# Linear attention block: denominators with heads on partitions, and reciprocals repeated by plain DMAs

## The chip, the cores and the metric

The kernel runs on one core of a Trainium2 chip. The metric is the device time of one execution in microseconds (us), as the median of several runs; lower is better.

## What is computed

An attention block and a feed-forward block, each behind a layer norm, with residuals. S = 2048 tokens, D = 512 features, 32 heads of 16 features, 1792 hidden features, all in bf16.

```
qkv = layernorm(x) @ wqkv
phi(t) = where(t > 0, t + 1, exp(t)) + 1e-6
kv  = einsum("bhsd,bhse->bhde", phi(k), v)
z   = sum of phi(k) over tokens
num = einsum("bhqd,bhde->bhqe", phi(q), kv)
den = einsum("bhqd,bhd->bhq", phi(q), z) + 1e-6
h   = x + (num / den) @ wo
out = h + relu(layernorm(h) @ w1) @ w2
```

The part at issue is 1 / den: one number for each token and head, by which all 16 features of that head are scaled.

## The kernel before

All tensors stay in SBUF. Tokens come in 16 tiles of 128 and in 4 chunks of 512 tokens. In the first third, each tile is normalized and transposed, K and the product G = ln^T phi(K) are accumulated over all tiles, and z is summed. Q is made transposed, with features on partitions: `pqT[c]` is 128 x 4 x 512, where the four blocks jb hold 8 heads of 16 features each. G, wv and wo are folded into one matrix `m_sb`, so attention's output is `h = x + (phi(q) / den) @ m_sb`. Then follow the hidden layer (`p` words, L510), its ReLU (`pA` on ACT, `pD` on VectorE) and the second product (`f` words, L530).

The order of everything is one list of words, `ORDER`, written out by hand: each word is an operation with its indices, the last one often a PSUM bank. Engines take their instructions in that order, and each waits for its data by semaphores; DMAs are issued by SP in that order too. A word that waits holds up all later words of its engine.

The denominators of a chunk c take this path. `zhd` holds z spread so that column q of block jb belongs to head q of that block (32 columns, of which 8 are not zero).

- `dn` (L443-451): sixteen matmuls with a 128 x 128 piece of `pqT[c]` as weights and 8 columns of `zhd` moving. Tokens come out on partitions, 128 numbers a partition.
- `dnl` (L453, ACT): Ln of these into `ld`.
- `dnx` (L459, ACT): Exp of minus that, read 16 times for each head, into `rn` (the memory of `wk_sb`), two token tiles at a time.
- `dt` (L478, SP): a transposing DMA for each token tile, from `rn` into `rd`, which then holds the reciprocal for each feature and token. Four a chunk. `rd` has room for one chunk.
- `dm` (L482, VectorE): `pqs = pqT * rd`, two blocks at once. It reads `rd` over all 512 tokens, so it needs all four transposes of the chunk.
- `h` (L490, L494, PE): four matmuls a token tile from `pqs` and `m_sb`; `hD` adds x.

Around chunk 1, SP's list goes on with a load of w2 (`l2.3.4`) and the transposes of `hn` (`x` words, L292), which the hidden layer needs.

Of the kernel before, what the change touches and what calls it, by code (L numbers as in the profile page):

```python
# [11 lines left out]
BF16 = mybir.dt.bfloat16  # L12
# [4 lines left out]

ORDER = """
const table lx.0.1 lx.2.1 S.0 lx.1.1 S.2 A.0 S.1 A.2 R.0.1 N.0 R.2.1 lx.3.1 lk.0.2 lx.4.2 masks warm.1.7
warm.9.7 A.1 R.1.1 T.0.6 S.3 warm.1.7 N.2 T.2.4 N.1 A.3 E.0 R.3.1 T.1.5 lk.2.2 S.4 E.1 N.3 A.4 V.2 S.5 A.5  # L20
K.0.6 lx.6.2 K.1.3 T.3.1 F.0.1 U.0.1 lx.8.4 E.3 K.2.0 M.0.1 S.6 D.0.1 K.3.2 A.6 S.7 F.1.1 M.1.1 lx.12.4 R.4.2
N.5 A.7 N.4 U.1.1 D.1.1 F.2.1 U.2.1 R.6.2 S.8 S.9 N.7 A.9 A.8 M.2.1 N.6 lq.0.2 G.0 T.5.1 E.5 T.4.3 G.1 X.7
K.5.1 D.2.1 E.4 K.4.0 R.8.2 T.6.3 G.2 N.9 X.9 F.3.1 U.3.1 S.12 N.8 S.13 X.8 lq.2.2 M.3.1 A.13 A.12 D.3.1 E.6
K.6.2 F.4.2 R.12.2 U.4.2 K.7.3 G.3 M.4.2 S.11 F.6.2 U.6.2 N.12 D.4.2 S.10 S.14 N.13 M.6.2 A.11 A.10 D.6.2 A.14
R.10.2 X.12 K.9.1 G.4 N.11 S.15 N.10 A.15 X.13 K.8.0 G.5 G.6 za.2 U.8.2 F.8.2 X.11 X.10 G.7 R.14.2 K.13.1
K.12.0 M.8.2 N.15 D.8.2 za.4 N.14 K.11.3 K.10.2 G.8 l2.0.3 F.12.2 U.12.2 za.6 X.15 X.14 Q.0.0.0 F.10.2 Q.0.1.1
lv.2.2 l1.0.2 M.12.2 lv.0.2 l2.10.4 U.10.2 qU.0.0.2 qF.0.0.2 M.10.2 za.8 D.12.2 D.10.2 za.10 za.12 K.14.2 G.9
K.15.3 F.14.2 U.14.2 G.10 Q.0.3.1 Q.0.2.0 M.14.2 qF.0.2.2 qU.0.2.2 G.11 zf.12 D.14.2 G.12 z.0.2.14 z.2.2.14
z.1.2.14 z.3.2.14 qM.0.2.2 l2.7.3 lo.0.2 lo.2.2 l1.2.2 qM.0.0.2 qD.0.2.2 G.13 zc G.14 qD.0.0.2 zh dn.0.0 G.15
gD.2.2 gD.0.2 Q.1.1.3 Q.1.0.2 dnl.0 dnx.0.0.2 Q.1.2.0 dnx.0.2.2 kv.3.4 kv.0.4 kv.1.4 kv.2.4 Q.1.3.1 qF.1.0.2  # L30
qM.1.0.2 kx qF.1.2.2 qW.1.0.2 dt.0 dt.3 dt.2 dt.1 m.2.6 m.1.5 m.3.7 m.0.4 mA.0.2 Q.2.0.2 Q.2.1.3 qM.1.2.2
mA.2.2 qW.1.2.2 dn.1.5 dm.0.0.2 dm.0.2.2 dnl.1 dnx.1.2.2 Q.2.3.1 h.3.5 hD.3 h.0.6 h.1.7 hD.0 s.3 dnx.1.0.2
dt.6 Q.2.2.0 dt.4 dt.7 dt.5 qF.2.0.2 qU.2.0.2 h.2.6 hD.1 Q.3.0.2 Q.3.1.3 s.0 qF.2.2.2 qU.2.2.2 s.1 qU.3.0.2
a.3 a.0 hD.2 qM.2.0.2 n.0 a.1 n.1 dm.1.0.2 dm.1.2.2 n.3 s.2 Q.3.2.0 Q.3.3.1 qD.2.0.2 a.2 qM.2.2.2 n.2 qF.3.0.2
qF.3.2.2 l2.3.4 x.0 qM.3.2.2 qD.2.2.2 h.5.6 h.7.7 h.6.5 x.1 t.2.3 r.0.4 e.2 h.4.4 x.3 dn.2.3 dnl.2 dnx.2.0.2
p.0.0.2 dt.8 hD.6 qM.3.0.2 qW.3.2.2 hD.4 p.0.1.3 qD.3.0.2 hD.5 dnx.2.2.2 pA.0.0.2 p.0.3.1 p.0.2.0 dn.3.6
pD.0.2.2 p.0.5.3 p.0.4.2 pD.0.4.2 p.0.7.1 p.0.6.0 p.0.13.3 s.6 dt.10 p.0.12.2 dt.11 dt.9 hD.7 a.6 s.5 dm.2.0.2
dm.2.2.2 dnl.3 pA.0.6.2 a.5 pD.0.12.2 f.2.6.0.7 s.7 h.11.7 h.9.0 p.0.9.3 h.8.5 p.0.8.2 dnx.3.2.2 dnx.3.0.2
hD.9 a.7 hD.11 p.0.10.0 f.3.7.0.7 p.0.11.1 h.10.4 dt.15 pA.0.10.2 pD.0.8.2 dt.14 dt.13 dt.12 s.4 s.9 n.5
dm.3.2.2 s.11 hD.8 a.11 dm.3.0.2 hD.10 n.7 f.2.6.7.7 h.13.5 h.15.4 n.6 hD.15 a.4 n.4 s.8 h.14.1 f.3.7.7.7  # L40
h.12.2 f.0.4.0.7 x.5 x.6 s.10 hD.14 a.10 hD.13 hD.12 n.10 x.4 s.13 s.12 x.7 n.11 a.9 a.8 f.1.5.0.7 a.12 s.15
p.1.1.1 p.1.0.0 pA.1.0.2 f.1.5.7.7 a.15 s.14 fo.2 p.1.8.0 p.1.9.1 n.12 a.13 fo.3 n.15 n.13 fo.1 pD.1.8.2
f.0.4.7.7 a.14 n.8 p.1.12.0 p.1.13.1 p.1.2.2 p.1.3.3 p.1.10.6 r.12.4 r.4.4 pA.1.12.2 n.9 x.11 x.15 x.10 x.9
x.8 pD.1.2.2 p.1.7.5 p.1.5.1 fd.2 fd.3 p.1.4.0 p.2.3.3 p.2.2.2 n.14 fo.0 pD.1.4.2 pD.2.2.2 fd.0 x.13 x.14
p.2.0.0 p.1.11.7 p.2.7.3 p.2.1.1 r.8.4 pA.2.0.2 p.2.6.2 p.1.6.4 pD.2.6.2 p.2.4.0 pA.1.10.2 pA.1.6.2 p.2.5.1
pA.2.4.2 f.7.7.0.7 p.2.12.0 p.2.13.1 f.4.4.0.7 f.5.5.0.7 p.2.10.2 f.4.4.7.7 p.2.11.3 f.6.6.0.7 pD.2.10.2
pD.2.12.2 fd.1 x.12 f.6.6.7.7 f.5.5.7.7 p.2.8.0 p.2.9.1 p.3.2.2 p.3.3.3 fo.6 pD.2.8.2 fo.4 fo.5 p.3.4.0
f.7.7.7.7 p.3.5.1 pA.3.4.2 pD.3.2.2 fo.7 f.10.6.0.7 p.3.1.1 f.9.5.0.7 p.3.7.3 p.3.0.0 f.8.4.0.7 p.3.6.2 fd.6
f.9.5.7.7 f.11.7.0.7 f.10.6.7.7 fd.4 fd.5 fd.7 pA.3.0.2 pA.3.6.2 f.8.4.7.7 p.3.12.0 fo.9 f.11.7.7.7 p.3.13.1
p.3.11.3 p.3.10.2 pD.3.10.2 fo.8 fo.11 pA.3.12.2 p.3.9.1 f.13.5.0.7 p.3.8.0 f.12.4.0.7 pA.3.8.2 fo.10 fd.10  # L50
fd.9 f.13.5.7.7 f.14.6.0.7 fo.13 f.12.4.7.7 f.15.5.0.14.3.1 f.14.6.7.7 f.15.7.0.14.0.2 fd.13 fd.8 fd.11 fo.12
fo.14 fo.15.3.1 f.15.4.0.14.2.1 fd.12 fd.14 fd.15.3.1 fo.15.0.2 fo.15.2.1 fd.15.0.2 fd.15.2.1
"""


# [1 line left out]
def kernel(  # L57
# [10 lines left out]
    nc = tc.nc  # L68
    P = 128
    xf = A_x.flatten_outer_dims()  # L70
    of = out.flatten_outer_dims()
    S, D = xf.shape
    FF = B_w1.shape[1]
    H = 32
    DH = D // H
    NT = S // P
    CW = 512
    CT = CW // P
    NCH = S // CW
    KD = D // P  # L80
    KF = FF // P
    Q4 = P // KD
    QH = P // DH
# [5 lines left out]
    big = ctx.enter_context(tc.tile_pool(name="big", bufs=1))  # L89
# [47 lines left out]
    rd = big.tile([P, 4, CW], BF16, name="rd")  # L137
    pqs = big.tile([P, NQ, CW], BF16, name="pqs")
    hn = big.tile([P, NQ, D], BF16, name="hn")
    o_t = gT  # L140
    r4 = rd
    rn = wk_sb
    z_acc = acts[1][:, 0:4, :].rearrange("p a n -> p (a n)").bitcast(F32).rearrange("p (a n) -> p a n", a=2)
    zeros = m_sb[:, 0, :]
# [281 lines left out]
    def op_dx4(c):  # L426
        nc.scalar.activation(out=r4[:, c, :], in_=ld[:, c % 2, :], func=ACT.Exp, scale=-1.0)

    def op_rp(c, jb, b):
        at_bank["rp", c, jb] = b  # L430
        rows = slice(jb * Q4, (jb + 1) * Q4)
        nc.tensor.matmul(
            bk[:, b, :], lhsT=erep[rows, :], rhs=r4[rows, c, :], start=True, stop=True
        )
# [146 lines left out]
```

## Time and profile before

| what | value |
|---|---|
| median of 3 runs | 169.91 us (169.65 to 170.24) |
| the profiled execution: span, first to last instruction | 168.6 us; no other time of this execution is listed |
| TensorE busy | 163.1 us, 97% |
| VectorE busy | 104.7 us, 62% |
| ACT busy | 64.3 us, 38% |
| mean granted clock of TensorE | 0.999 |

In the rows of the timeline the first number is the start and the second the length, both in us; then follow engine, line, operation, operands, shapes and the number of instructions merged, and in brackets how long the engine was idle before and what ended that. PEld is the load of weights, which runs beside PE. In the chain of waits the columns are start, length and what the time went to. In a group's row, the columns behind the count are busy us and mean ns of one, and then the idle time before. In a row of one source line, three numbers with slashes are least, median and greatest ns. In a row by windows stand the window's length, the busy time of each engine with its instructions, the granted clock, the mean busy share of the 16 DMA engines, and GB/s.

### The profile page before, as it was taken

How to read it: one execution, taken by the hardware profiler on the slowest of the kernel's cores; microseconds unless marked ns; L12 is line 12 of the kernel's file. 1: busy time of each engine (PE TensorE's matmuls, PEld its weight loads, DVE VectorE, ACT ScalarE, POOL GpSimd, SP SyncE). 2: the span in 40 equal slices, each digit the busy share in tenths (PEclk: the TensorE clock that was granted, in tenths of full speed). 3: DMA queues.
4: the chain of work that ended last, by engine and by line, in shares of the span. 5: the costliest groups of instructions: out<-in, count | busy, mean ns of one | idle time of the engine just before them, and what ended most of it. 6: DMA issues, size and time to landing. Idle time of an engine off the chain costs nothing.

```text
span 168.6 us, 2307 instructions
## 1 busy us (share of the span) xinstructions
PE 163.1 (97%) x875; PEld 76.3 (45%) x875; DVE 104.7 (62%) x207; ACT 64.3 (38%) x97; POOL 4.8 (3%) x21
## 2 busy tenths in 40 slices
PE   7799999999999999999999999999999999999993
PEld 2354444444554354444444444444444444444463
DVE  3999999996879896978799725220066401007132
ACT  3699867775589755600201140170000203021000
POOL 7400000000000000000000000000000000000000
PEclk9999999999999999999999999999999999999999
DMA  4972847896414653232142343400000200000232
GB/s 130 295 254 47 146 79 176 312 365 230 95 31 93 156 97 79 45 74 50 41 83 40 62 90 100 91 4 0 0 0 31 93 4 0 0 0 0 79 111 62
DMA packets 30091, 15.36 MB, mean 91 GB/s; under 512 B 22656, under 2 KB 29056, under 8 KB 30080
## 3 DMA queue, kind: packets, MB, share of 16 engines
q1 hardware_dynamic: 30080, 15.21, 34.6%
q8 instruction: 7, 0.11, 0.3%
q14 instruction: 4, 0.03, 0.1%
HBM read 7.86 MB, written 2.10 MB: 59 GB/s over the span
## 4 chain that ended last, share of the span: by engine, by line
PE 84%; ACT 4%; DMA 4%; SPq 3%; DVE 2%; issue 1%; DVEq 0%; ACTq 0%
PE bk L530 29%; PE bk L510 29%; PE bk L351 7%; PE bk L299 7%; PE bk L494 6%; PE bk L307 5%; DMA wk_sb<-in_A_wqkv_dram 3%; ACT eb L317 1%; DMA rd<-wk_sb 1%; SPq L201 1%; SPq L480 1%; PE bk L448 1%; ACT rb L320 1%; DVE pqT L332 1%; ACT lnT L280 1%
## 5 line engine op out<-in xcount | busy, mean ns | idle before, releaser
L530 PE MATMUL bk<-w_sb,at 128*128 128x512 bf16 (+2 forms) x252 | 51.5, 355 | 0.0
L510 PE MATMUL bk<-lnT,w_sb 128*128 128x512 bf16 x224 | 51.4, 379 | 0.0
L516 ACT ACTIVATE at<-bk 128x1024 bf16<-128x1024 f32 x14 | 14.1, 1023 | 70.3 <-PE bk L510 70.3
L521 DVE TENSOR_SCALAR at<-bk 128x1024 bf16<-128x1024 f32 x14 | 17.0, 1221 | 33.7 <-PE bk L510 33.7
L530 PEld LDWEIGHTS <-at 128*128 128x128 bf16 x252 | 23.6, 98 | 25.2
L510 PEld LDWEIGHTS <-w_sb 128*128 128x128 bf16 x224 | 21.8, 98 | 26.0 <-issue 0.2
L538 DVE SCALAR_TENSOR_TENSOR gT<-bk,rstd,h_nat 128x512 bf16<-128x512 f32 (+2 forms) x18 | 12.0, 686 | 18.3 <-PE bk L530 15.9
L317 ACT ACTIVATE eb<-bk 128x1024 bf16<-128x1024 f32 (+1 forms) x18 | 16.5, 925 | 6.1 <-PE bk L299 3.5
L299 PE MATMUL bk<-wk_sb,lnT 128*128 128x512 bf16 x64 | 15.5, 379 | 0.6 <-DMA wk_sb<-in_A_wqkv_dram 0.5
L494 PE MATMUL bk<-m_sb,pqs 128*128 128x512 bf16 x64 | 15.5, 379 | 0.1
L307 PE MATMUL bk<-lnT,wq_sb 128*128 128x512 bf16 x64 | 15.1, 379 | 0.1
L320 ACT ACTIVATE rb<-bk 128x1024 bf16<-128x1024 f32 (+1 forms) x15 | 13.6, 906 | 1.2 <-PE bk L307 1.2
L351 PE MATMUL bk<-at,h_nat 128*128 128x512 bf16 x56 | 13.7, 379 | 0.0
L500 DVE TENSOR_TENSOR h_nat<-bk,x_nat 128x512 bf16<-128x512 f32 x16 | 10.8, 678 | 2.7 <-PE bk L494 2.6
L226 DVE BATCH_NORM_STATS2 st<-x_nat 128x6 f32<-128x512 bf16 x16 | 10.6, 678 | 1.8 <-DMA x_nat<-in_A_x_dram 1.8
L228 DVE BATCH_NORM_STATS2 st<-h_nat 128x6 f32<-128x512 bf16 x16 | 10.5, 679 | 0.0
L299 PEld LDWEIGHTS <-lnT 128*128 128x128 bf16 x64 | 5.9, 98 | 8.2 <-ACT lnT L280 1.2
L494 PEld LDWEIGHTS <-pqs 128*128 128x128 bf16 x64 | 6.1, 98 | 7.9 <-DVE pqs L484 1.2
L307 PEld LDWEIGHTS <-wq_sb 128*128 128x128 bf16 x64 | 6.1, 97 | 7.3 <-issue 0.4
L351 PEld LDWEIGHTS <-h_nat 128*128 128x128 bf16 x64 | 6.0, 98 | 6.6
L461 ACT ACTIVATE wk_sb<-ld 128x1024 bf16<-128x1024 f32 x8 | 8.0, 1048 | 0.1
L324 DVE TENSOR_SCALAR eb<-eb 128x1024 bf16<-128x1024 bf16 (+1 forms) x18 | 6.9, 388 | 1.2 <-ACT eb L317 1.1
(57 smaller groups left out, 90.3 us busy)
## 6 DMA issues: line engine op xcount, KB each, us to landing
out_dram<-gT SPq DMA_DIRECT2D x15, 128.0 KB, 1.8
w_sb<-in_B_w_dram SPq DMA_DIRECT2D x2, 896.0 KB, 6.7
x_nat<-in_A_x_dram SPq DMA_DIRECT2D x2, 512.0 KB, 7.8
w_sb<-in_B_w_dram SPq DMA_DIRECT2D x2, 512.0 KB, 5.2
w_sb<-in_B_w_dram SPq DMA_DIRECT2D x2, 384.0 KB, 5.1
x_nat<-in_A_x_dram SPq DMA_DIRECT2D x4, 128.0 KB, 2.2
wk_sb<-in_A_wqkv_dram SPq DMA_DIRECT2D x2, 256.0 KB, 3.7
x_nat<-in_A_x_dram SPq DMA_DIRECT2D x2, 256.0 KB, 4.1
```

The source lines that it names most:

```text
L299: nc.tensor.matmul(bk[:, b, :], lhsT=lnT[c][:, kd, j * P : (j + 1) * P], rhs=wk_sb[:, kd, :], start=(kd == 0), stop=(kd == KD - 1),)
L307: nc.tensor.matmul(bk[:, b, :], lhsT=wq_sb[:, kd, j * P : (j + 1) * P], rhs=lnT[c][:, kd, :], start=(kd == 0), stop=(kd == KD - 1),)
L317: nc.scalar.activation(out=buf(eb, kind, i, n), in_=bank(at_bank[kind, i], n), func=ACT.Exp)
L320: nc.scalar.activation(out=buf(rb, kind, i, n), in_=bank(at_bank[kind, i], n), func=ACT.Relu)
L351: nc.tensor.matmul(bk[:, KD + kd, :], lhsT=ln_nat[:, t, kd * P : (kd + 1) * P], rhs=pk(t)[:, 0, :], start=(t == 0), stop=(t == NT - 1),)
L494: nc.tensor.matmul(bk[:, b, :], lhsT=pqs[:, (c * KD + jb) % NQ, j * P : (j + 1) * P], rhs=m_sb[:, jb, :], start=(jb == 0), stop=(jb == KD ...
L500: nc.vector.tensor_tensor(out=h_nat[:, t : t + n, :], in0=bank(at_bank["h", t], n), in1=x_nat[:, t : t + n, :], op=ALU.add,)
L510: nc.tensor.matmul(bk[:, b, cols], lhsT=w1_sb[:, kd, f * P : (f + 1) * P], rhs=lnT[c][:, kd, cols], start=(kd == 0), stop=(kd == KD - 1),)
L516: nc.scalar.activation(out=acts[c % 2][:, f : f + n, :], in_=bank(at_bank["p", c, f], n), func=ACT.Relu)
L521: nc.vector.tensor_scalar(out=acts[c % 2][:, f : f + n, :], in0=bank(at_bank["p", c, f], n), scalar1=0.0, scalar2=None, op0=ALU.max,)
L530: nc.tensor.matmul(bk[:, b, 0 : w * P], lhsT=acts[c % 2][:, f, j * P : (j + 1) * P], rhs=w2_sb[:, f, k * P : (k + w) * P], start=(f == 0), ...
L538: nc.vector.scalar_tensor_tensor(out=o_t[:, t % NO, cols], in0=bk[:, at_bank["f", t, k], 0 : w * P], scalar=rstd2[:, t : t + 1], in1=h_nat ...
```

## The change

Four operations take the place of the five above, and the words of ORDER are replaced where they stood; nothing else is moved.

- `d4` for `dn`: four matmuls a chunk, one for each block, with 32 columns of `zhd` as weights and 512 columns of `pqT[c]` moving. Block jb's result goes to partitions 32 jb to 32 jb + 31 of one bank: heads on partitions (8 of each 32 are used), tokens along the row.
- `dl4` for `dnl`: Ln of 128 x 512.
- `dx4` for the two `dnx`: Exp of minus that, 128 x 512, into `r4`, which is now a tile of its own with room for all four chunks.
- `bc` for `dt`: a plain DMA for each block, from the 8 rows of `r4` that hold its heads, each read 16 times, into `rd[:, jb, :]`.

`dm` is as before, but the two blocks that it reads need two of the four DMAs of its chunk.

```diff
-    r4 = rd
+    r4 = big.tile([P, NCH, CW], BF16, name="r4")
...
+    def op_bc(c, jb):
+        src = r4[jb * Q4 : jb * Q4 + QH, c, :].rearrange("p (o n) -> p o n", o=1)
+        nc.sync.dma_start(out=rd[:, jb, :], in_=src.broadcast_to([QH, DH, CW]))
```

The words replaced in ORDER, with a word beside each that stays:

```diff
 zh
-dn.0.0
+d4.0.0
 Q.1.0.2
-dnl.0 dnx.0.0.2 Q.1.2.0 dnx.0.2.2
+dl4.0 dx4.0 Q.1.2.0
 qW.1.0.2
-dt.0 dt.3 dt.2 dt.1
+bc.0.0 bc.0.3 bc.0.2 bc.0.1
 qW.1.2.2
-dn.1.5 dm.0.0.2 dm.0.2.2 dnl.1 dnx.1.2.2
+d4.1.5 dm.0.0.2 dm.0.2.2 dl4.1 dx4.1
 s.3
-dnx.1.0.2 dt.6 Q.2.2.0 dt.4 dt.7 dt.5
+bc.1.2 Q.2.2.0 bc.1.0 bc.1.3 bc.1.1
 x.3
-dn.2.3 dnl.2 dnx.2.0.2 p.0.0.2 dt.8
+d4.2.3 dl4.2 dx4.2 p.0.0.2 bc.2.0
 ...
-dn.3.6
+d4.3.6
 s.6
-dt.10 p.0.12.2 dt.11 dt.9
+bc.2.2 p.0.12.2 bc.2.3 bc.2.1
 dm.2.2.2
-dnl.3
+dl4.3
 p.0.8.2
-dnx.3.2.2 dnx.3.0.2
+dx4.3
 h.10.4
-dt.15 pA.0.10.2 pD.0.8.2 dt.14 dt.13 dt.12
+bc.3.3 pA.0.10.2 pD.0.8.2 bc.3.2 bc.3.1 bc.3.0
```

More of the change, by code (lines that the diff above doesn't have):

```diff
@@ L19 @@
 const table lx.0.1 lx.2.1 S.0 lx.1.1 S.2 A.0 S.1 A.2 R.0.1 N.0 R.2.1 lx.3.1 lk.0.2 lx.4.2 masks warm.1.7
[L20 to L52, printed above, removed]
+warm.9.7 A.1 R.1.1 T.0.6 S.3 warm.1.7 N.2 T.2.4 N.1 A.3 E.0 R.3.1 T.1.5 lk.2.2 S.4 E.1 N.3 A.4 V.2 S.5 A.5 K.0.6
@@ new lines @@
+lx.6.2 K.1.3 T.3.1 F.0.1 U.0.1 lx.8.4 E.3 K.2.0 M.0.1 S.6 D.0.1 K.3.2 A.6 S.7 F.1.1 M.1.1 lx.12.4 R.4.2 N.5 A.7
+N.4 U.1.1 D.1.1 F.2.1 U.2.1 R.6.2 S.8 S.9 N.7 A.9 A.8 M.2.1 N.6 lq.0.2 G.0 T.5.1 E.5 T.4.3 G.1 X.7 K.5.1 D.2.1
+E.4 K.4.0 R.8.2 T.6.3 G.2 N.9 X.9 F.3.1 U.3.1 S.12 N.8 S.13 X.8 lq.2.2 M.3.1 A.13 A.12 D.3.1 E.6 K.6.2 F.4.2
+R.12.2 U.4.2 K.7.3 G.3 M.4.2 S.11 F.6.2 U.6.2 N.12 D.4.2 S.10 S.14 N.13 M.6.2 A.11 A.10 D.6.2 A.14 R.10.2 X.12
+K.9.1 G.4 N.11 S.15 N.10 A.15 X.13 K.8.0 G.5 G.6 za.2 U.8.2 F.8.2 X.11 X.10 G.7 R.14.2 K.13.1 K.12.0 M.8.2 N.15
@@ new lines @@
+D.8.2 za.4 N.14 K.11.3 K.10.2 G.8 l2.0.3 F.12.2 U.12.2 za.6 X.15 X.14 Q.0.0.0 F.10.2 Q.0.1.1 lv.2.2 l1.0.2
+M.12.2 lv.0.2 l2.10.4 U.10.2 qU.0.0.2 qF.0.0.2 M.10.2 za.8 D.12.2 D.10.2 za.10 za.12 K.14.2 G.9 K.15.3 F.14.2
+U.14.2 G.10 Q.0.3.1 Q.0.2.0 M.14.2 qF.0.2.2 qU.0.2.2 G.11 zf.12 D.14.2 G.12 z.0.2.14 z.2.2.14 z.1.2.14 z.3.2.14
+qM.0.2.2 l2.7.3 lo.0.2 lo.2.2 l1.2.2 qM.0.0.2 qD.0.2.2 G.13 zc G.14 qD.0.0.2 zh d4.0.0 G.15 gD.2.2 gD.0.2
+Q.1.1.3 Q.1.0.2 dl4.0 dx4.0 Q.1.2.0 kv.3.4 kv.0.4 kv.1.4 kv.2.4 Q.1.3.1 qF.1.0.2 qM.1.0.2 kx qF.1.2.2 qW.1.0.2
@@ new lines @@
+bc.0.0 bc.0.3 bc.0.2 bc.0.1 m.2.6 m.1.5 m.3.7 m.0.4 mA.0.2 Q.2.0.2 Q.2.1.3 qM.1.2.2 mA.2.2 qW.1.2.2 d4.1.5
+dm.0.0.2 dm.0.2.2 dl4.1 dx4.1 Q.2.3.1 h.3.5 hD.3 h.0.6 h.1.7 hD.0 s.3 bc.1.2 Q.2.2.0 bc.1.0 bc.1.3 bc.1.1
+qF.2.0.2 qU.2.0.2 h.2.6 hD.1 Q.3.0.2 Q.3.1.3 s.0 qF.2.2.2 qU.2.2.2 s.1 qU.3.0.2 a.3 a.0 hD.2 qM.2.0.2 n.0 a.1
+n.1 dm.1.0.2 dm.1.2.2 n.3 s.2 Q.3.2.0 Q.3.3.1 qD.2.0.2 a.2 qM.2.2.2 n.2 qF.3.0.2 qF.3.2.2 l2.3.4 x.0 qM.3.2.2
+qD.2.2.2 h.5.6 h.7.7 h.6.5 x.1 t.2.3 r.0.4 e.2 h.4.4 x.3 d4.2.3 dl4.2 dx4.2 p.0.0.2 bc.2.0 hD.6 qM.3.0.2
@@ new lines @@
+qW.3.2.2 hD.4 p.0.1.3 qD.3.0.2 hD.5 pA.0.0.2 p.0.3.1 p.0.2.0 d4.3.6 pD.0.2.2 p.0.5.3 p.0.4.2 pD.0.4.2 p.0.7.1
+p.0.6.0 p.0.13.3 s.6 bc.2.2 p.0.12.2 bc.2.3 bc.2.1 hD.7 a.6 s.5 dm.2.0.2 dm.2.2.2 dl4.3 pA.0.6.2 a.5 pD.0.12.2
+f.2.6.0.7 s.7 h.11.7 h.9.0 p.0.9.3 h.8.5 p.0.8.2 dx4.3 hD.9 a.7 hD.11 p.0.10.0 f.3.7.0.7 p.0.11.1 h.10.4 bc.3.3
+pA.0.10.2 pD.0.8.2 bc.3.2 bc.3.1 bc.3.0 s.4 s.9 n.5 dm.3.2.2 s.11 hD.8 a.11 dm.3.0.2 hD.10 n.7 f.2.6.7.7 h.13.5
+h.15.4 n.6 hD.15 a.4 n.4 s.8 h.14.1 f.3.7.7.7 h.12.2 f.0.4.0.7 x.5 x.6 s.10 hD.14 a.10 hD.13 hD.12 n.10 x.4 s.13
@@ new lines @@
+s.12 x.7 n.11 a.9 a.8 f.1.5.0.7 a.12 s.15 p.1.1.1 p.1.0.0 pA.1.0.2 f.1.5.7.7 a.15 s.14 fo.2 p.1.8.0 p.1.9.1 n.12
+a.13 fo.3 n.15 n.13 fo.1 pD.1.8.2 f.0.4.7.7 a.14 n.8 p.1.12.0 p.1.13.1 p.1.2.2 p.1.3.3 p.1.10.6 r.12.4 r.4.4
+pA.1.12.2 n.9 x.11 x.15 x.10 x.9 x.8 pD.1.2.2 p.1.7.5 p.1.5.1 fd.2 fd.3 p.1.4.0 p.2.3.3 p.2.2.2 n.14 fo.0
+pD.1.4.2 pD.2.2.2 fd.0 x.13 x.14 p.2.0.0 p.1.11.7 p.2.7.3 p.2.1.1 r.8.4 pA.2.0.2 p.2.6.2 p.1.6.4 pD.2.6.2
+p.2.4.0 pA.1.10.2 pA.1.6.2 p.2.5.1 pA.2.4.2 f.7.7.0.7 p.2.12.0 p.2.13.1 f.4.4.0.7 f.5.5.0.7 p.2.10.2 f.4.4.7.7
@@ new lines @@
+p.2.11.3 f.6.6.0.7 pD.2.10.2 pD.2.12.2 fd.1 x.12 f.6.6.7.7 f.5.5.7.7 p.2.8.0 p.2.9.1 p.3.2.2 p.3.3.3 fo.6
+pD.2.8.2 fo.4 fo.5 p.3.4.0 f.7.7.7.7 p.3.5.1 pA.3.4.2 pD.3.2.2 fo.7 f.10.6.0.7 p.3.1.1 f.9.5.0.7 p.3.7.3 p.3.0.0
+f.8.4.0.7 p.3.6.2 fd.6 f.9.5.7.7 f.11.7.0.7 f.10.6.7.7 fd.4 fd.5 fd.7 pA.3.0.2 pA.3.6.2 f.8.4.7.7 p.3.12.0 fo.9
+f.11.7.7.7 p.3.13.1 p.3.11.3 p.3.10.2 pD.3.10.2 fo.8 fo.11 pA.3.12.2 p.3.9.1 f.13.5.0.7 p.3.8.0 f.12.4.0.7
+pA.3.8.2 fo.10 fd.10 fd.9 f.13.5.7.7 f.14.6.0.7 fo.13 f.12.4.7.7 f.15.5.0.14.3.1 f.14.6.7.7 f.15.7.0.14.0.2
@@ L53 @@
+fd.13 fd.8 fd.11 fo.12 fo.14 fo.15.3.1 f.15.4.0.14.2.1 fd.12 fd.14 fd.15.3.1 fo.15.0.2 fo.15.2.1 fd.15.0.2
+fd.15.2.1
 """
```

## The prediction

> **What bounds the kernel now.** I read the page first: busy shares, clock, chain.
>
> ```profile
> span 168.6 us, 2307 instructions
> ...
> PE 163.1 (97%) x875; PEld 76.3 (45%) x875; DVE 104.7 (62%) x207; ACT 64.3 (38%) x97; POOL 4.8 (3%) x21
> ...
> PEclk9999999999999999999999999999999999999999
> ...
> PE 84%; ACT 4%; DMA 4%; SPq 3%; DVE 2%; issue 1%; DVEq 0%; ACTq 0%
> ```
>
> TensorE is the bound at full clock. ACT is busy 38%, so work saved there is worth nothing by itself. What leaves the chain for DMA and SP must be a stretch where the denominators are late. The chain in order of time and the timeline of PE and VectorE show where; these are the denominator matmuls (L448), the last transpose of chunk 1, and the products and h matmuls that wait for them.
>
> ```profile
> 39.58 0.38 PE bk L448 x16
> ...
> 48.14 0.49 PE bk L448 x16
> ...
> 54.04 2.43 DMA rd<-wk_sb
> ...
> 61.36 0.38 PE bk L448 x16
> ...
> 65.22 0.38 PE bk L448 x16
> ```
>
> ```profile
> 49.34 2.75 PE L494 MATMUL bk<-m_sb,pqs 128*128 128x512 bf16 x12
> 53.65 3.62 PE L307 MATMUL bk<-lnT,wq_sb 128*128 128x512 bf16 x16
> 57.34 2.94 PE L494 MATMUL bk<-m_sb,pqs 128*128 128x512 bf16 x12
> 72.14 1.89 PE L494 MATMUL bk<-m_sb,pqs 128*128 128x512 bf16 x8
> 82.07 2.75 PE L494 MATMUL bk<-m_sb,pqs 128*128 128x512 bf16 x12
> ```
>
> ```profile
> 48.25 1.29 DVE L484 TENSOR_TENSOR pqs<-pqT,rd 128x1024 bf16<-128x1024 bf16 x2 [0.20 <-DMA rd<-wk_sb]
> 56.59 1.29 DVE L484 TENSOR_TENSOR pqs<-pqT,rd 128x1024 bf16<-128x1024 bf16 x2 [0.46 <-DMA rd<-wk_sb]
> 70.45 1.27 DVE L484 TENSOR_TENSOR pqs<-pqT,rd 128x1024 bf16<-128x1024 bf16 x2
> 81.13 0.66 DVE L484 TENSOR_TENSOR pqs<-pqT,rd 128x1024 bf16<-128x1024 bf16 x1
> ```
>
> Sixteen matmuls take 3.62 us and twelve 2.75, so four more cost 0.87: 0.217 us per 512 columns, and 2.75 less 12 of these leaves a tail of 0.15 in which the last one empties. At 53.65 sixteen matmuls end streaming at 57.10, but the next starts at 57.34, and its twelve take 2.94 instead of 2.75. So late reciprocals cost PE 0.24 + 0.19 = 0.43 us in chunk 1. In chunk 0 VectorE waited 0.20 and PE did not; in chunks 2 and 3 VectorE did not wait. The reciprocals are already just in time: faster ones win 0.43 us at most, slower ones cost nearly their whole delay, because VectorE and PE work in a fixed order and everything behind the product waits with it.
>
> **Denominators on PE.** Removed: four groups L448, 0.38 + 0.49 + 0.38 + 0.38 = 1.63 us. Added per chunk: four matmuls of 512 columns, each into its own 32 output partitions. No row of this trace shows such a matmul. Bounds: all four at once, 0.22; one after another, 0.87, or 1.17 if the array empties before and after (twice the tail of 0.15). I take at once but with both tails, 0.52, since a change of shape that cannot overlap its neighbours is the nearest reading of that tail: 4 x 0.52 = 2.08, or +0.45 us; the ends are -0.76 and +3.05. [...]
>
> **Logarithm and exponential on ACT.**
>
> ```profile
> 40.00 0.37 ACT L454 ACTIVATE ld<-bk,eps 128x128 f32<-128x128 f32 x1 [2.30 <-PE bk L448]
> 48.65 0.37 ACT L454 ACTIVATE ld<-bk,eps 128x128 f32<-128x128 f32 x1 [0.51 <-PE bk L448]
> 61.78 0.37 ACT L454 ACTIVATE ld<-bk,eps 128x128 f32<-128x128 f32 x1 [0.65 <-PE bk L448]
> L461 ACT ACTIVATE wk_sb<-ld 128x1024 bf16<-128x1024 f32 x8 | 8.0, 1048 | 0.1
> L317 ACT ACTIVATE eb<-bk 128x1024 bf16<-128x1024 f32 x14 | 14.2, 1021 | 5.2 <-PE bk L299 2.6 <-PE bk L307 2.5
> L317 ACT ACTIVATE eb<-bk 128x512 bf16<-128x512 f32 x4 | 2.4, 589 | 0.9 <-PE bk L299 0.9
> ```
>
> From the last two rows 512 elements cost 0.43 us, 0.84 ns each. The new Ln has 512 columns instead of 128: 0.37 + 384 x 0.84 ns = 0.69 us. The new Exp has 512 instead of 1024: 1.05 - 0.43 = 0.61. Together 1.30 per chunk against 0.37 + 2 x 1.05 = 2.47. ACT saves 1.2 us a chunk, covered by its own slack. The Ln holds its PSUM bank 0.32 us longer; in chunk 1 the first h matmuls write the same bank (5), and the four Q matmuls between (0.87 us) still cover 0.69. Without them it would cost up to 0.2. The first repeat of a chunk can be issued at 40.00 + 1.30 = 41.3, 49.95 and 63.1 in chunks 0 to 2.
>
> **The repeats, which decide.**
>
> ```profile
> L480 SPq DMA_TRANSPOSE rd<-wk_sb x16: 1189/1212/1265, 41.5 to 75.7; - x16
> ...
> DMA to landing us min/median/max: 2.4/2.5/2.8
> L201 SPq DMA_DIRECT2D x_nat<-in_A_x_dram x8: 400/430/468, 0.8 to 5.1; - x8
> 36.00:38.00 2.00, 2.00 (x25) 1.15 (x24) 2.00 (x5) 1.70 (x2) 0.00 (x0) 1.00 1.10 348
> ```
>
> Removed: 16 transposes, each 1.21 us of SP. Added: 16 plain copies of the same 128 KB into the same tile, at about 0.43 us of SP (L201). The queue is freed earlier for what stands behind it (the w2 load and the transposes of hn), which have slack. But each copy reads its 128 KB from 8 partitions, sixteen times each. Call the interval from one landing to the next r. Low bound: 0.43 (issue; at 348 GB/s the bytes alone need 0.38). High bound: if a partition gives no more than its share of the full rate, 348/128 = 2.7 GB/s, eight give 22 and a copy takes 6.0. The ends are far apart. The nearest row is the one for the same bytes into the same tile inside SBUF: 2.5 us from issue to landing. I take r = 2.5, with nothing of one copy hidden behind another, because all four of a chunk run in one queue and each draws on few partitions. The transposes could overlap, as each read all 128. [...]
>
> Now the sum, with the fourth copy landing 4r = 10 us after the start. Chunk 0: products need copies 0 and 1, issued first and last: landed at 51.3, product over at 51.95 (half of 1.29), h at 52.0 instead of 49.34: +2.7. The second product ends at 52.6. Chunk 1: copies overwrite rd, so they start then: last landed at 62.6, against 56.59: +6.0, the first 2.7 included. Chunk 2: start 63.1 + 6.0 = 69.1, landed 79.1, h at 79.8 against 72.14 + 6.0 = 78.1: +1.7, now 7.7. Chunk 3: start 80.4 when the product of chunk 2 has read rd, landed 90.4, h at 91.05 against 82.07 + 7.7 = 89.8: +1.3. Sum +9.0. The extra PE time in chunks 0 and 1 is hidden by these stalls; in chunks 2 and 3 it adds 2 x (0.52 - 0.38) = 0.3. So the span becomes 168.6 + 9.3 = 177.9; the median of the runs shown, 169.91, stands 1.3 above the profiled span, so 179.2 us. The same steps give +2.0 with r = 2.0 and +17 with r = 3.0: this case's own range is 172 to 187.
>
> **The rivals.** The turning point follows from chunk 1: 49.95 + 4r = 56.59 at r = 1.66. Below that, no copy is late, the 0.43 us is won, and PE's own work decides.
> - Repeats early, four matmuls truly at once, no tail: -0.76 - 0.43 = -1.2, 168.7 us, faster. For it: plain copies from HBM go at 348 GB/s and the queue is empty when the copies start. Against it: those read all partitions.
> - Repeats early, matmuls at once with tails: +0.45 - 0.43, 169.9, no change.
> - The four matmuls do not run together, so the change does not do what it says: +1.85 - 0.43 = +1.4, 171.3 (172.5 with tails), slower for PE alone. For it: every matmul of this trace streams one after another at 0.217.
>
> **How the numbers follow.** Late repeats 0.47 (179.2); early with tails 0.19 (169.9); one after another 0.16 (171.3); at once 0.15 (168.7); 0.03 is left for r near 6, far above 187. A measurement of this kernel can tell about 0.3%, 0.5 us, from no change. Faster: 0.15 and a little of the second rival, 0.17. Same: most of the second, 0.16. Slower: 0.67. Cases of both signs hold much of the chance, so the range runs from 168.7 to 187, leaving out some faster repeats of the first rival and the slowest copies.
>
> **What would show it.** VectorE's L484 should wait for DMA rd<-r4 by microseconds in chunks 0, 1, 2 and 3, with PE gaps before L494 at each, and landings that climb by 2 to 3 us through the four copies of a chunk. If landings stay at 2 to 4 us, the forecast is wrong and one of the rivals holds: then the distance from the first denominator matmul to PE's next other matmul (0.22, 0.52, 0.87 or 1.17) says which. A clock below full, or a late load or transpose behind the copies in SP's queue, would be none of these.

## The result, and the profile after

The change makes the kernel slower: 183.6 us against 170.06 in the same runs (6 each), ratio 1.0784, 95% interval 1.0741 to 1.0827. Two of the six runs took 186.7 and 187.4 us and the other four 183.4 to 183.7, and the ratio is that of the four. The forecast was 179.2, so its direction and mechanism hold, but it put the loss at 9.3 us where 13.5 were lost.

The page of the kernel after:

```profile
span 181.7 us, 2185 instructions
...
PE 164.8 (91%) x812; PEld 74.9 (41%) x827; DVE 104.7 (58%) x207; ACT 60.2 (33%) x93; POOL 4.8 (3%) x21
...
PEclk9999999999978999999999999999999999999999
...
PE 66%; DMA 18%; SPq 7%; DVE 3%; issue 2%; ACT 1%; DVEq 0%
```

PE is busy for 164.8 us, nearly as before, in a span that is 13.1 longer. DMA's part of the chain went from 4% to 18%, SP's from 3% to 7%. Two of the 40 slices, from 50.0 to 59.1 us, have a lower TensorE clock, of which more below.

VectorE's products and the h matmuls that follow them, with PE's first denominators, in the timeline after:

```profile
38.88 0.40 PE L416 MATMUL bk<-pqT,zhd 128*32 128x512 bf16 x4
...
39.21 1.04 PE L351 MATMUL bk<-at,h_nat 128*128 128x512 bf16 x4
...
51.75 1.29 DVE L488 TENSOR_TENSOR pqs<-pqT,rd 128x1024 bf16<-128x1024 bf16 x2 [4.28 <-DMA rd<-r]
...
52.50 0.57 PE L498 MATMUL bk<-m_sb,pqs 128*128 128x512 bf16 x1 [3.62 <-DVE pqs L488]
...
53.29 3.66 PE L498 MATMUL bk<-m_sb,pqs 128*128 128x512 bf16 x10 [0.22 <-DVE pqs L488]
...
62.96 1.29 DVE L488 TENSOR_TENSOR pqs<-pqT,rd 128x1024 bf16<-128x1024 bf16 x2 [1.93 <-DMA rd<-r]
...
80.63 1.29 DVE L488 TENSOR_TENSOR pqs<-pqT,rd 128x1024 bf16<-128x1024 bf16 x2 [3.65 <-DMA rd<-r]
...
81.38 2.07 PE L498 MATMUL bk<-m_sb,pqs 128*128 128x512 bf16 x8 [2.63 <-DVE pqs L488]
...
94.48 0.69 DVE L488 TENSOR_TENSOR pqs<-pqT,rd 128x1024 bf16<-128x1024 bf16 x1 [3.19 <-DMA rd<-r]
...
95.23 2.12 PE L498 MATMUL bk<-m_sb,pqs 128*128 128x512 bf16 x9 [3.58 <-DVE pqs L488]
```

In every chunk VectorE waits for the copies, 13.6 us in all, and PE waits behind it, 11.6 us in all. The chain in order of time shows the copies of chunk 0:

```profile
40.71 0.81 SPq L431
...
41.57 0.61 SPq L431
...
42.23 1.91 SPq L431
...
44.18 7.55 DMA rd<-r
```

SP issues the first copy at 40.71; the fourth lands at 51.73, 11.0 us later. The third and fourth issue themselves take 1.9 and 2.5 us. While data move, 42.1 to 51.4, the row by windows reads (last two columns: busy share of the 16 DMA engines, GB/s):

```profile
42.10:51.40 9.30, 6.69 (x44) 2.94 (x42) 4.44 (x6) 6.98 (x8) 0.00 (x0) 1.00 0.41 59
```

59 GB/s, of which some 3 are two loads of instructions, so 56 for the copies, where loads of all partitions gave 348 (kernel before, 36 to 38 us). A packet of 1 KB took 144 ns in the median of these 512 packets, against 46 for the loads of both kernels.

### The profile page after: what moved, and what is told of

The parts are those of the page before. It is cut to its first block, busy times and chain, and to the rows that moved or that the text cites. A ratio compares the mean times of both kernels' runs of the same rounds, so it can differ in the third digit from the quotient of the medians.

```text
span 181.7 us, 2185 instructions
## 1 busy us (share of the span) xinstructions
PE 164.8 (91%) x812; PEld 74.9 (41%) x827; DVE 104.7 (58%) x207; ACT 60.2 (33%) x93; POOL 4.8 (3%) x21
## 4 chain that ended last, share of the span: by engine, by line
PE 66%; DMA 18%; SPq 7%; DVE 3%; issue 2%; ACT 1%; DVEq 0%
PE bk L534 24%; PE bk L514 20%; DMA rd<-r 17%; PE bk L299 8%; PE bk L351 7%; SPq L431 7%; PE bk L498 4%; PE bk L307 2%; DVE pqs L488 2%; DMA x_nat<-in_A_x_dram 1%; PE bk L270 1%; DVE st L226 1%; ACT ld L422 1%; ACT r L427 1%; PE bk L416 0%
## 5 line engine op out<-in xcount | busy, mean ns | idle before, releaser
L534 PE MATMUL bk<-w_sb,at 128*128 128x512 bf16 (+2 forms) x246 | 50.9, 355 | 0.3
L498 PE MATMUL bk<-m_sb,pqs 128*128 128x512 bf16 x62 | 16.9, 409 | 11.7 <-DVE pqs L488 11.6
L317 ACT ACTIVATE eb<-bk 128x1024 bf16<-128x1024 f32 (+1 forms) x18 | 16.5, 925 | 13.1 <-PE bk L307 10.3
L498 PEld LDWEIGHTS <-pqs 128*128 128x128 bf16 x64 | 6.1, 104 | 21.6 <-DVE pqs L488 14.8
L320 ACT ACTIVATE rb<-bk 128x1024 bf16<-128x1024 f32 (+1 forms) x15 | 13.6, 905 | 1.2 <-PE bk L307 1.2
L351 PE MATMUL bk<-at,h_nat 128*128 128x512 bf16 x55 | 13.7, 379 | 0.1
L488 DVE TENSOR_TENSOR pqs<-pqT,rd 128x1024 bf16<-128x1024 bf16 x8 | 5.3, 689 | 13.6 <-DMA rd<-r 13.6
L232 ACT ACTIVATE rstd<-mv,eps 128x2 f32<-128x2 f32 (+2 forms) x14 | 4.1, 295 | 10.1 <-DVE mv L229 6.2
```

Of the source, the lines that this page charges most:

```text
L317: nc.scalar.activation(out=buf(eb, kind, i, n), in_=bank(at_bank[kind, i], n), func=ACT.Exp)
L320: nc.scalar.activation(out=buf(rb, kind, i, n), in_=bank(at_bank[kind, i], n), func=ACT.Relu)
L351: nc.tensor.matmul(bk[:, KD + kd, :], lhsT=ln_nat[:, t, kd * P : (kd + 1) * P], rhs=pk(t)[:, 0, :], start=(t == 0), stop=(t == NT - 1),)
L498: nc.tensor.matmul(bk[:, b, :], lhsT=pqs[:, (c * KD + jb) % NQ, j * P : (j + 1) * P], rhs=m_sb[:, jb, :], start=(jb == 0), stop=(jb == KD ...
L534: nc.tensor.matmul(bk[:, b, 0 : w * P], lhsT=acts[c % 2][:, f, j * P : (j + 1) * P], rhs=w2_sb[:, f, k * P : (k + w) * P], start=(f == 0), ...
```

## The experiments

**Which property of the copies is slow.** Four kernels change only the source of the copies (and, where said, the mask).

E1 reads every partition of r4 once:

```diff
-        src = r4[jb * Q4 : jb * Q4 + QH, c, :].rearrange("p (o n) -> p o n", o=1)
-        nc.sync.dma_start(out=rd[:, jb, :], in_=src.broadcast_to([QH, DH, CW]))
+        nc.sync.dma_start(out=rd[:, jb, :], in_=r4[:, c, :])
```

> Each copy reads all 128 partitions of r4 once instead of 8 rows sixteen times; bytes, count, queue, order and waits stay, but the values in rd are not the reciprocals wanted. Theory A (a copy is limited by the few partitions it reads): the 144 to 147 ns that a 1 KB packet takes in the changed kernel falls back to about 46, the fourth copy of a chunk lands within 4 us of the first issue instead of 11, VectorE never waits for rd, and the time is about 169.5 us (PE's denominators cost the same as before, 0.41 against 0.41 us a chunk, and the 0.43 us gap in chunk 1 goes). Theory B (SP's issue, the single queue, or the single rd buffer is the limit): nothing here touches those, so 183 us stays.

Measured: 169.63 us, ratio 0.9969 (0.9942 to 0.9996). Copies in one queue, issued by SP, into a single rd, are not slow in themselves: theory B falls, A holds so far.

E2 spreads the heads over the 32 rows that the matmul writes anyway, and reads every fourth:

```diff
-        keep(mask_h[:], mask_h[:], [[0, KD], [-DH, Q4]], 0, 1)
-        keep(mask_h[:], mask_h[:], [[0, KD], [DH, Q4]], DH - 1, -1)
+        mask_d = mask_h.rearrange("p k (q r) -> p k q r", r=Q4 // QH)
+        keep(mask_d, mask_d, [[0, KD], [-DH, QH], [0, Q4 // QH]], 0, 1)
+        keep(mask_d, mask_d, [[0, KD], [DH, QH], [0, Q4 // QH]], DH - 1, -1)
...
-        src = r4[jb * Q4 : jb * Q4 + QH, c, :]
+        src = r4[jb * Q4 : (jb + 1) * Q4 : Q4 // QH, c, :]
```

> The mask is widened so that each head's denominator comes out on 4 neighbouring partitions, and each copy reads 8 rows that lie 4 partitions apart, still sixteen times each: same number of source rows, of repeats and of bytes for each row. Theory A (the limit belongs to groups of neighbouring partitions that share a path): eight groups instead of two, so four times the rate, copies land in time, about 169.5 us. Theory C (the limit is the eight rows themselves: so many engines, or so many re-reads of one row): unchanged, packets near 145 ns and about 183 us.

Measured: 170.22 us, ratio 0.9993 (0.9968 to 1.0019). Eight rows, each read sixteen times, and the loss is gone; packets are back at 46 ns. So the eight rows and their re-reading are not the limit; that they are neighbours is. Its SP row for the copies, and VectorE's product in chunk 1, which waits for nothing:

```profile
L432 SPq DMA_DIRECT2D rd<-r x16: 607/607/812, 41.4 to 73.6; - x16
...
56.16 1.29 DVE L489 TENSOR_TENSOR pqs<-pqT,rd 128x1024 bf16<-128x1024 bf16 x2
```

The long issues, up to 2.5 us, are gone too, so they came from slow copies ahead in the queue and were not the cause.

E3 (16 neighbouring rows, eight times each) and E4 (all 32 rows, four times each) use the same mask:

```diff
+        src = r4[jb * Q4 : jb * Q4 + 16, c, :]   # E3, to [16, 8, CW]
+        src = r4[jb * Q4 : jb * Q4 + 32, c, :]   # E4, to [32, 4, CW]
```

> Each copy reads 16 neighbouring rows eight times (values in rd are not those wanted). Theory A: twice the groups of the changed kernel, so 1.2 us a copy, 4.7 us for the four data phases of a chunk, the last landing some 6.5 us after the first issue, just in time for chunk 1 (6.2 us are there): 169.5 to 170.5 us, and about 110 GB/s while copies run. Theory C (engines or re-reads): also in time, but at 200 GB/s or more while copies run.

> With the widened mask of the run before last, each copy reads all 32 rows of its block, each four times: the result is that of the reference. Theory A: eight groups and all engines, 0.6 us a copy, all four landed within 4 us; 169.5 us, that is 0.2 to 0.3% below the kernel before, since PE's denominators cost as before and only the 0.43 us gap in chunk 1 goes. Theory B: 183 us.

Measured: E3 169.9 us, ratio 0.998 (0.9957 to 1.0004); E4 169.99 us, ratio 0.9986 (0.9964 to 1.0007). Both are in time, so only the rate tells the theories of E3 apart. The data of a chunk, from the first to the last packet's start, take 4.8 us in E3 in each of chunks 0, 2 and 3, close to the 4.7 that theory A forecast; that is 109 GB/s. The rows by windows, taken inside chunk 3 while copies run, are of the kernel after, E3, E1, E2 and E4, in this order:

```profile
83.50:87.50 4.00, 4.00 (x20) 1.86 (x19) 2.90 (x6) 0.00 (x0) 0.00 (x0) 1.00 0.45 48
...
73.00:75.00 2.00, 2.00 (x11) 0.94 (x10) 1.38 (x4) 0.00 (x0) 0.00 (x0) 1.00 0.91 96
...
72.50:74.50 2.00, 2.00 (x11) 0.90 (x10) 1.39 (x4) 0.00 (x0) 0.00 (x0) 1.00 0.62 210
...
73.00:75.00 2.00, 2.00 (x11) 0.90 (x10) 1.38 (x4) 0.00 (x0) 0.00 (x0) 1.00 0.53 185
...
72.50:74.50 2.00, 2.00 (x11) 0.88 (x9) 1.39 (x4) 0.00 (x0) 0.00 (x0) 1.00 0.84 196
```

By the order of the copies and this rate, the window of the kernel after holds rows of one half alone, those of blocks 3 and 2. Eight neighbouring rows give 48 GB/s and sixteen give 96. With 32 rows, or eight rows four apart, the rate is 185 to 196, and there it is close to what the issues allow, since a copy of 128 KB every 0.65 to 0.7 us is 187 to 202 GB/s. In E3 the DMA engines are busy 0.91 of the time and move no more than half of what E1 moves at 0.62, so a lack of engines is not what limits it. That is theory A: the rate doubles with the number of neighbouring rows, 48 to 96, and eight rows four apart read at 185. The size of such a group of neighbours, and which engines a copy uses, are suppositions of the expectations that no run shows; four apart is the only spacing that was tried.

E4 computes the reference's result and undoes the loss, but does not beat the kernel before: the interval holds 1. Its landings and the product of chunk 1:

```profile
DMA to landing us min/median/max: 2.5/2.7/4.0
...
55.61 1.29 DVE L489 TENSOR_TENSOR pqs<-pqT,rd 128x1024 bf16<-128x1024 bf16 x2
...
56.60 2.75 PE L499 MATMUL bk<-m_sb,pqs 128*128 128x512 bf16 x12
```

PE's twelve matmuls take 2.75 us and follow without a gap: the 0.43 us of the prediction is won in the profile, but with an interval 0.7 us wide it does not show beyond doubt.

**How four copies add up.** E5 lets ACT issue the copies of blocks 2 and 3, E10 does so right behind the exponential, E9 keeps SP's queue and alternates the halves.

```diff
-        nc.sync.dma_start(out=rd[:, jb, :], ...)
+        (nc.scalar if jb >= 2 else nc.sync).dma_start(out=rd[:, jb, :], ...)   # E5, E10
```

```diff
-bc.0.0 bc.0.3 bc.0.2 bc.0.1
+bc.0.0 bc.0.2 bc.0.1 bc.0.3   # E9; chunk 2 alike, chunk 3: 2 0 3 1
-dx4.0
+dx4.0 bc.0.2 bc.0.3           # E10, each chunk alike
```

> The changed kernel, but the copies of blocks 2 and 3 are issued by ACT, those of 0 and 1 by SP. Blocks 0 and 1 lie in rows 0 to 7 and 32 to 39, blocks 2 and 3 in rows 64 to 71 and 96 to 103. Theory A1 (a narrow path for each pair of blocks, and a single queue in which the next copy cannot pass the one in front): the two pairs now run beside each other, the last copy of a chunk lands after about 6.5 us instead of 11, and the time falls to 170 to 172 us. Theory A2 (all copies share one limit of some 56 GB/s, whichever rows they read): the last still lands after 11 us, 183 us or a little more, since ACT now also issues.

> The changed kernel; only the order of the four copies of chunks 0, 2 and 3 is changed, so that no two neighbours in the queue read rows of the same half (blocks 0 and 1 read the first 64 partitions, 2 and 3 the others): 0 2 1 3, and 2 0 3 1 in chunk 3. Chunk 1 had such an order already. Theory A1 (each pair of blocks has its own narrow path, and a copy on the other path overlaps the tail of the one in front): the data phase of chunks 0 and 2 shrinks from 9.3 us to about 7, that of chunk 3 from 10.8 to about 7, and the copies that the first product needs are there with the third: 176 to 179 us. Theory A2 (one limit of some 56 GB/s for all): the phases stay, and the time falls only by what the first product gains, to 182 or 183 us.

> As the run with two queues, but ACT issues the copies of blocks 2 and 3 right behind the exponential that they read, so both pairs really start together (in that run ACT issued them 4 us later, when the first pair was half through). Theory A1: the pairs run beside each other, packets still at 145 ns or so but twice as many in a microsecond, the last copy lands 6.5 us after the start; 170 to 173 us. Theory A2: 183 us or more.

Measured: E5 184.94 us (ratio 1.0825, 1.0751 to 1.09). Its time tells nothing about A1: ACT, working in order, issued its copies in chunk 0 at 46.1 and 47.4, after SP's at 42.1 and 43.0, and in chunk 3 its last one at 88.5. Only in chunk 2 did both queues start together, at 71.1 and 71.6, and there the data took 7.5 us. E9 177.94 (1.043, 1.0343 to 1.0516), inside what A1 forecast, though the data stay above its 7 us. The data of a chunk, from the first to the last packet's start, take 7.7, 7.8 and 8.1 us in chunks 0, 2 and 3, against 9.2, 9.4 and 10.8 in the kernel after (chunk 1 is left out, since packets of w2 run among its own). The window of chunk 0 in E9:

```profile
42.70:50.40 7.70, 6.73 (x45) 2.98 (x44) 5.12 (x7) 5.66 (x7) 0.00 (x0) 1.00 0.42 71
```

So the halves do overlap, and A2 falls; chunk 3 of the kernel after was the worst because its order, 3 2 1 0, changes halves only once. E10 178.11 (1.044, 1.0372 to 1.0508), and the expected halving did not come: 8.4, 7.7 and 7.5 us. Two queues overlap no better than a good order in one. The trace shows part of why. In chunk 2 both queues issue their first copy at 67.91, yet from 69.1 to 71.4 every packet is of ACT's queue (q10); the two mix only later. The first line below is the queue's packets, MB and busy share in that time; the others are rows by windows before and during the mixing:

```profile
q10 hardware_dynamic: 107, 0.11, 43.4%
...
69.50:71.50 2.00, 2.00 (x13) 0.75 (x12) 1.32 (x2) 1.43 (x2) 0.00 (x0) 1.00 0.44 46
74.00:75.00 1.00, 1.00 (x6) 0.47 (x5) 1.00 (x4) 1.00 (x2) 0.00 (x0) 1.00 0.50 120
```

So the pairs did not start beside each other even here. The cause stays open: the busy share of the 16 engines is 0.42 to 0.50 in all these rows, and no run shows which engines each queue uses.

**The single rd.** E7 gives rd room for two chunks; the copies and products of chunk c use its half c % 2:

```diff
-    rd = big.tile([P, 4, CW], BF16, name="rd")
+    rd = big.tile([P, 8, CW], BF16, name="rd")
...
```

> The changed kernel with room for two chunks in rd, so that the copies of a chunk need not wait until the product of the chunk before has read rd. Rate and rows of the copies stay. Theory F (the single rd adds to what the rate costs): chunk 1 gains 1.9 us (its copies follow those of chunk 0 without a pause, then VectorE's own order is next) and chunk 3 gains 3.7: 178.0 us. Theory G (the rate alone decides): 183.5 us.

Measured: 179.97 us (1.0534, 1.0458 to 1.061), span 177.7. Theory F holds, with 4.0 us of span instead of 5.6. The waits of chunks 1 and 3 are gone, those of chunks 0 and 2 stay (products of chunks 1, 2 and 3, and the h matmuls of chunk 2):

```profile
61.29 1.28 DVE L488 TENSOR_TENSOR pqs<-pqT,rd 128x1024 bf16<-128x1024 bf16 x2
...
78.77 1.29 DVE L488 TENSOR_TENSOR pqs<-pqT,rd 128x1024 bf16<-128x1024 bf16 x2 [3.42 <-DMA rd<-r]
...
79.52 3.34 PE L498 MATMUL bk<-m_sb,pqs 128*128 128x512 bf16 x8 [2.40 <-DVE pqs L488]
...
88.42 0.68 DVE L488 TENSOR_TENSOR pqs<-pqT,rd 128x1024 bf16<-128x1024 bf16 x1
```

PE's waits for these products fall by 5.3 us, from 11.6 to 6.3, nearly the forecast. The difference to 4.0 fits a second stretch of slow clock: eight h matmuls of chunk 2 take 3.34 us, where the kernel after needed 2.07, and no later stall hides it.

**The slow clock.** After the 3.62 us stall of chunk 0, ten h matmuls took 3.66 us instead of 2.3; seven starts lie 427 ns apart, where 216 is usual. The granted clock is 0.5 from 52.6 to 56.0 us. E6, and E11 in more rounds, fill that stall:

```diff
-Q.2.3.1 h.3.5
+Q.2.3.1 warm.15.5 h.3.5
```

> The changed kernel with 15 matmuls of no use (3.25 us) put before the first h matmul of chunk 0, where PE idled 3.8 us and then ran seven matmuls at 427 ns apart instead of 217. Theory D (that slow stretch costs its 1.6 us): 182.0 us. Theory E (the stretch is hidden, because the copies of chunk 1 land at the same time and VectorE waited 1.93 us for them anyway): no change, 183.5 us, with VectorE's wait in chunk 1 longer by about 1.6.

> The run with 15 matmuls of no use in chunk 0 again, in more rounds. Theory D: 182.0 us. Theory E: no gain over the changed kernel's 183.6, since the wait moves into chunk 1 (VectorE waited 3.47 us there in the first look instead of 1.93), and the slow clock moves there with it.

Measured: E6 184.62 and 188.85 us; E11 185.23 (1.0837, 1.0761 to 1.0913). D falls. E's reading of the wait holds: in E11 the h matmuls of chunk 0 run at full speed and VectorE waits in chunk 1 for 3.45 us instead of 1.93, for copies that land when they did.

```profile
52.84 2.93 PE L498 MATMUL bk<-m_sb,pqs 128*128 128x512 bf16 x12 [0.35 <-DVE pqs L488]
...
63.33 1.29 DVE L488 TENSOR_TENSOR pqs<-pqT,rd 128x1024 bf16<-128x1024 bf16 x2 [3.45 <-DMA rd<-r]
...
64.08 4.50 PE L498 MATMUL bk<-m_sb,pqs 128*128 128x512 bf16 x12 [3.13 <-DVE pqs L488]
```

The slow stretch moved there: twelve matmuls in 4.50 us. In the kernel after, the slow stretch of chunk 0 costs nothing of its own, since the copies of chunk 1 are waited for in any case. That the stalls bring the slow clock about is argued: in the traces of the kernel after, E5, E7 and E11, each of its six stretches begins within a stall of PE or less than 1 us behind one, and E1 to E4 and E8, which have no such stall, have none. But stalls of up to 2.97 us in E9 and 2.68 in E10 brought none either.

**PE's denominators.** E8 issues each group of four twice in the kernel of E4:

```diff
-        for jb in range(KD):
+        for jb in [*range(KD), *range(KD)]:
```

> The kernel with 32 source rows, but each group of four denominator matmuls is issued twice in a row into the same place (the result stays that of the reference). Theory H (four column groups work at once, and most of the 0.41 us of a group is the change into and out of that mode, paid once for both): +0.22 us a chunk, +0.9 in all, 170.8 us. Theory I (each group pays all): +1.7, 171.6. Theory J (the four run one after another): +0.87 a chunk, +3.5, 173.4.

Measured: 170.83 us, ratio 1.0025 (0.9993 to 1.0057), beside 0.9986 for E4. Theory H:

```profile
39.58 0.61 PE L417 MATMUL bk<-pqT,zhd 128*32 128x512 bf16 x8
40.13 0.82 PE L352 MATMUL bk<-at,h_nat 128*128 128x512 bf16 x3
```

Eight matmuls of 512 columns take 0.61 us where four take 0.40; eight in sequence would need 1.7. From the start of the matmul ahead of the group to that of the matmul behind it are 0.64 us with four and 0.86 with eight. Less the 0.22 of the matmul ahead, a group of four delays PE by 0.42 us and one of eight by 0.64: 0.22 for each set of four at once, and 0.21 besides, paid once for both sets, as theory H has it. What these 0.21 us go to no row shows.

## Why the prediction was right, and where it was short

- **Late repeats decide** (0.47): right. VectorE waits for DMA rd<-r in all four chunks, PE before L498 at each, and E1, E2 and E4 remove the loss by the source rows alone. The three rivals with early repeats did not come about; E1 to E4, where the repeats are early, come to 169.6 to 170.2 us, about the second rival's 169.9.
- **r = 2.5 us:** too small, and the one term that carries the error. From the first issue to the fourth landing it took 11.0, 9.8, 11.1 and 12.5 us, not 10. The prediction's own steps with these four in place of 10 give delays of 3.7, 6.8, 9.6 and 13.4 us and, with its 0.3 and 1.3 added, 183.6 us. The landings of the single copies do not stand in the trace of this kernel, so that they climb by 2 to 3 us was not seen. Measured against the kernel before, with 0.54 us that this run was ahead at the first denominators, the h matmuls after chunks 0 to 3 are late by 3.7, 6.9, 9.8 and 13.7 us; forecast were 2.7, 6.0, 7.7 and 9.0. Chunk 3 failed most: +3.9 instead of +1.3, because its copies stand in the order that overlaps least. There "nothing of one copy hidden behind another" was nearly right, and the price was too low: 128 KB at the 48 GB/s of one half are 2.7 us, and four of these the 10.8 measured. In chunks 0 and 2 some of it was hidden; what is hidden depends on the order.
- **The row chosen for r**, 2.5 us from a transpose's issue to its landing, is not the interval between two copies: four copies need 1.4 us from the first issue to the first packet (42.1 - 40.7, chunk 0), paid once, and then 2.3 us of data each in chunk 0 (9.2 / 4), where copies overlap, and 2.7 in chunk 3 (10.8 / 4). That 2.5 lies between these two is chance.
- **From span to time**, 1.3: this compared two executions. A run's time stands 1.75 us above its own span (183.45 and 181.7), so the same sum would have come to 179.6.
- **The single rd** as amplifier: right; with room for two chunks (E7) PE waits 5.3 us less and the span is 4.0 shorter.
- **Denominators on PE:** four at once, as taken, but 0.42 instead of 0.52, so +0.02 a chunk instead of +0.1: beside the 0.22 of the matmuls stand 0.21 rather than two tails of 0.15. The new Ln took 0.69 and the Exp 0.63, as worked out (0.69, 0.61).
- **SP's issue at 0.43:** wrong, 0.61 at best in this kernel and 2.5 when the queue backs up; nothing hung on it.
- **The clock:** named as a sign against the forecast; it came behind the stalls, with the forecast mechanism at work.

## What to carry to other kernels

Before a copy repeats few SBUF rows, ask how many rows it reads and how they lie: here eight neighbours gave 48 GB/s, sixteen 96, and eight rows four apart 185. The 512 KB of a chunk (0, 2 and 3) took 9.2 to 10.8 us from eight neighbours at a time, and at most 4.2 from 32 rows (chunk 0 of E4, 42.1 to 46.3 at 131 GB/s). Here the producer could write the same values to more partitions at no cost that shows (E4, ratio 0.9986), since 24 of 32 matmul columns were idle. And where a buffer holds one round only, a slow transfer is paid in each round, since the next may not start until the last consumer has read; room for two rounds took 4.0 us off the span (E7).

## What had not been expected of the hardware

- Copies on different halves of the partitions overlap in part in one queue if they alternate: 7.7 us against 9.2 for the same four copies in chunk 0, and 8.1 against 10.8 in chunk 3. A second queue added little or nothing (7.5 to 8.4).
- An SP issue takes longer when copies are slow: 0.61 to 2.54 us in the kernel after, the longest as the third or fourth of a chunk, where E2 had 0.61 to 0.81.
- PE stalls of 2.40 us (E7, chunk 2), 3.13 (E11, chunk 1) and 3.62 (after, chunk 0) were followed by a slow clock, but not those of 2.63 and 3.58 in chunks 2 and 3 after, nor one of 2.97 in E9. The length of the stall alone does not decide it.
